# Token rows for the final mixing, x turned first, xT loaded later, and stages of its own for step 0

## The chip, the cores and the metric

The kernel runs on one core of a Trainium2 chip. Its time is the device time of one execution in microseconds (us), and the figure compared is the median over runs. Five engines run their own instruction streams and meet through semaphores: TensorE (PE, with its weight loads as PEld), VectorE (DVE), ScalarE (ACT), GpSimd (POOL) and SyncE (SP), which here only issues DMAs. ACT and POOL issue DMAs as well. The DMA engines, 16 in the profile, carry all transfers.

## The reference

Two branches read the same x (2048 tokens of 1024) and are mixed token by token with a gate `g`. Branch A walks over 64 segments of 32 tokens and carries a memory of 8 rows from segment to segment. Branch B is a GELU-gated feed-forward layer with 3584 hidden columns.

```python
def _A_ref(x, mem0, Wq, Wk, Wv, Wo, seg_len):
    ...
    for s in range(n_seg):
        xs = x[:, s * seg_len:(s + 1) * seg_len, :].copy()
        h = jnp.concatenate([mem, xs], axis=1)
        q = jnp.einsum('btd,dhe->bhte', h, Wq)   # k and v alike; 32 heads of 128
        ...
        scores = jnp.where(mask[None, None], scores, -1000000000.0)
        p = _softmax(scores, axis=-1)
        o = jnp.einsum('bhqk,bhke->bhqe', p, v)
        o = jnp.einsum('bhte,hed->btd', o, Wo)
        mem = o[:, :M, :].copy()
        outs.append(o[:, M:, :])

def _B_ref(x, w_gate, w_up, w_down):
    return _gelu(x @ w_gate) * (x @ w_up) @ w_down
g = _sigmoid((x * gate_w).sum(-1, keepdims=True))
return g * a + (1 - g) * b
```

## The kernel before

The program is a list of operations in one order, written by hand. Each operation goes to one engine; its waits are worked out from the regions that it reads and writes, and each engine runs its own in the order of the list. A DMA has a lane, and a DMA waits for the one before it on its lane. PSUM has 8 banks; two engines that touch the same bank are kept in the order of the list. On-chip memory is laid out by hand in slots of 4 KB a partition, counted by `edge(n)` from 0 to 49, and tiles of different phases share them.

**Head and branch B.** x comes in 16 tiles of 128 tokens (`px`, four buffers). `do_x(T)` turns a tile on TensorE (L550), copies the result to `xT` or `xq` in halves by ACT and DVE (L557, L558), copies the last 8 rows of each segment by DVE (L559), writes both to memory (`xq_scr`, `xr_scr`), and then lets GpSimd multiply the tile with the gate's weights into `gp` (L566) and DVE sum the product (L568). `gate(fb)` makes the gate of four tiles and writes it out, to `g_scr` and, 4 bytes to a row, to `gt_scr` (L636). `load_h` fetches a segment's turned x into `hT`, the input of the recurrence, and a DVE copy puts the memory rows beside it (L663).

The four token blocks `fb` of 512 tokens each have 28 column blocks `j`: 8 matmuls for the gate and 8 for the up projection (L680), then Square and Tanh on ACT (L688, L692) and three operations on DVE (L689, L693, L696). Column block j uses PSUM banks that block j-2 must have left. The gate and up weights come in five chunks `c` of 2, 5, 7, 7 and 7 column blocks (`load_w`). Then comes the down projection, two passes `ps` over seven weight tiles `wd` of 1 MB (L732), 16 matmuls to a tile. The tiles have three buffers: `load_wd` for the tile three ahead is issued when a tile is used up. In the last block all seven tiles, `wdF`, are loaded ahead. `mix` scales the result by 1-g and writes it to `b_scr`. `load_xT(fb+1)` (L594) fetches the next block's 1 MB of turned x. `begin(n)` loads a slot of the recurrence's weights for the first time, and `spread` copies weights within memory.

**The recurrence.** 64 steps, each with the projections k, q, v and the output projection o in two halves of the heads, r = 0 and 1, each in eight pieces n. The walk over (m, r, n) is a list, and `on(m, r, n, f)` hangs work in front of a piece. Weights do not all fit, so `spent` has SP reload the pieces that share a slot. The last 8 rows of each segment and the memory both go through "rest" projections: `fill` (L986) projects the last rows of four segments at a time, `fill_evac` copies the result to a stage by ACT and for v writes it to `v_scr` (L997), and `fill_put` turns it (L814), copies it by DVE (L1009) and writes it to `qk_scr` from GpSimd (L1011, one lane, `fq`). `load_qk` and `load_v` (L581, L585) bring a step's share back, and `put_rest` (L1015) copies it into `kT`. `scores` (L839 to L862) makes the softmax, `attend` (L874) applies it and `rest_o` (L899) collects the rest rows of the output, which go to `o_scr`. A stage is a place under a working tile: stage "k" is kT's, "q" is qT's, "o" is oT's, 0 and 1 lie under hT and oRc. The weights o are `wall`, all others `sl`. After the last output piece `fold` adds the two halves of PSUM: a DVE copy of 64x256 to `part` (L960) and a DVE sum (L961); then TensorE turns the memory rows for the next step (L970). The folded result goes from GpSimd to `a_scr`.

**The mixing.** `oR` holds the rest rows of all steps, four blocks of 1 MB; TensorE multiplies each with Wo (L1157), and DVE adds the gated sum (L1167). For each of 16 token tiles `load_a` fetches branch A's rows from `a_scr` in four DMAs of 96 x 256 (L780) and branch B's from `b_scr` in one (L782); `blend` sums them on DVE (L789) and ACT writes the result (L792). There are six buffers of each (`NA`), and tile T+5 is asked for after tile T's sum.

Of the kernel before, what the change touches and what calls it, by code (L numbers as in the profile page):

```python
# [5 lines left out]
BF16 = mybir.dt.bfloat16  # L6
# [204 lines left out]
def bass_gated_mix__memory_aug_recurrent_mem_tr__geglu_ffn__prompt_kernel(  # L211
# [34 lines left out]
    with ExitStack() as es:  # L246
# [16 lines left out]
        a_scr = nc.dram_tensor("a_scr", [NSEG, 4, SEG, 256], BF16)  # L263
# [254 lines left out]
        assert cur[0] == edge(50) and len(hosts) == 50  # L518
        tp = [al(f"tp{t}", [128, FB], FP32, at=qkr.off + 4 * FB * t) for t in range(2)]
# [21 lines left out]
        def do_x(T):  # L541
# [21 lines left out]
            if T > 0:  # L563
                op("act", lambda e: e.dma_start(xr_scr[T], to.rearrange("p k i c -> p (k i c)")),
                   rd=[to_r], wr=[("D", "xr", T)], lane=f"xv{x2}")
            op("pool", lambda e: e.tensor_tensor(out=gp[:, :], in0=t[:, :], in1=gwb[:, :], op=ALU.mult),  # L566
# [87 lines left out]
        load_w(1)  # L654
        for T in range(TB):
            do_x(T)
            load_x(T + NPX)
        gate(0)
# [3 lines left out]
        load_h(0, "pool")  # L662
        op("dve", lambda e: e.tensor_copy(hT0[:, :, NR:32], memT[:, :].rearrange("p (k c) -> p k c", k=KC)),  # L663
           rd=[memT.r()], wr=[hT0.r()])
# [84 lines left out]
        oR = [al(f"oR{b}", [128, RB, 32], at=slots[home["q", 0, 0]].off + b * SB * 512) for b in range(NBK)]  # L749
# [7 lines left out]
        NA = 6  # L757
# [6 lines left out]
        assert cur[0] <= slots[home["v", 1, 5]].off  # L764
# [12 lines left out]
        def load_a(T):  # L777
            t, w = asb[T % NA], bsb[T % NA]
            for n in range(4):
                op("sp", lambda e, n=n: e.dma_start(t[0:NM, 256 * n:256 * n + 256], a_scr[4 * T:4 * T + 4, n, 0:NR, :]),  # L780
                   rd=[("D", "a", s) for s in range(4 * T, 4 * T + 4)], wr=[t.r(256 * n, 256 * n + 256)], lane=f"al{T % NA}{n}")
# [427 lines left out]
```

## Time and profile before

| | us |
|---|---|
| median of 3 runs | 2300.27 |
| lowest and highest | 2295.94, 2300.56 |
| the profiled execution | 2304.75 |
| its span, first to last instruction | 2302.9 |
| TensorE busy | 2051.2 (89%) |
| DVE, ACT, POOL busy | 1042.1, 539.0, 434.2 |
| mean granted TensorE clock | 0.965 |

The span is read in stretches: head and branch B until about 650 us, the recurrence until about 2180, the mixing until the end. In the profile's rows, a timeline row has start, length, engine, line, operation, what it writes and reads, count, and in brackets how long the engine had been idle and what ended that; a letter q behind an engine's name means its instruction queue, as in SPq for the DMAs that SyncE issues.

### The profile page before, as it was taken

The numbers are of one execution on the slowest core, as the hardware profiler recorded it, in microseconds if no ns is written. First come the engines' busy times: TensorE is split into PE (matmuls) and PEld (weight loads), VectorE is DVE, ScalarE is ACT, GpSimd is POOL, SyncE is SP. The second block draws the span as 40 slices with busy tenths as digits, with TensorE's granted clock in tenths as the row PEclk, the third lists the DMA queues.
The fourth block names the chain that finished last, engine by engine and source line by source line (L and its number), as shares of the span: only waits on it lengthen the run. The fifth ranks groups of instructions, "written<-read, shape, count | busy, mean of one in ns | idle before, by whom it ended". The sixth has DMA issues, their size and how long they took to land.

```text
span 2302.9 us, 69850 instructions
## 1 busy us (share of the span) xinstructions
PE 2051.2 (89%) x31365; PEld 975.8 (42%) x31365; DVE 1042.1 (45%) x2689; ACT 539.0 (23%) x1110; POOL 434.2 (19%) x839
## 2 busy tenths in 40 slices
PE   5999989999968999899999999999999989998880
PEld 2444434444424444444444444444444444444450
DVE  3624606516314445454545454555454544544412
ACT  2312303203112222222222222222222222222100
POOL 3000100000012222222222222222223222221100
PEclk8999999999989999999999999999999999998895
DMA  9255385293577899899999898999999989998932
GB/s 302 107 169 193 107 248 166 59 320 118 188 282 281 329 345 350 330 349 346 346 342 350 330 350 330 358 347 361 351 351 335 349 327 345 342 348 321 345 121 99
DMA packets 187871, 652.74 MB, mean 283 GB/s; under 512 B 22156, under 2 KB 78092, under 8 KB 146740
## 3 DMA queue, kind: packets, MB, share of 16 engines
q1 hardware_dynamic: 161060, 608.10, 72.6%
q0 software_dynamic: 14528, 26.32, 3.5%
q10 hardware_dynamic: 11984, 13.85, 1.7%
q8 instruction: 246, 4.03, 0.7%
q14 instruction: 53, 0.43, 0.1%
HBM read 613.64 MB, written 49.23 MB: 288 GB/s over the span
## 4 chain that ended last, share of the span: by engine, by line
PE 62%; DMA 21%; DVE 6%; SPq 5%; ACT 3%; issue 2%; POOL 1%; ACTq 0%; DVEq 0%; POOLq 0%
PE pb L916 24%; PE pb L680 13%; DMA wall<-o_scr 10%; PE pb L732 7%; PE pb L932 5%; PE pb L814 3%; SPq L780 3%; PE pb L949 3%; DMA o_scr<-oRc 3%; PE pb L986 2%; DMA wd<-in_B_w_down_dram 2%; DMA sl<-v_scr 1%; DVE oT L800 1%; PE pb L874 1%; DMA qk_scr<-1S 1%
## 5 line engine op out<-in xcount | busy, mean ns | idle before, releaser
L916 PE MATMUL pb<-sl,hT 128*32 128x512 bf16 x12288 | 763.9, 384 | 15.1 <-DVE hT L973 8.8
L916 PEld LDWEIGHTS pb<-sl,hT 128*32 128x32 bf16 x12288 | 308.5, 97 | 326.7 <-issue 27.7
L680 PE MATMUL pb<-xT,wg 128*128 128x512 bf16 x896 | 215.2, 384 | 21.8 <-DVE GT L696 15.6
L986 PE MATMUL pb<-sl,hR 128*32 128x512 bf16 x3072 | 212.9, 385 | 3.2 <-DVE osb L621 1.5
L680 PE MATMUL pb<-xT,wu 128*128 128x512 bf16 x896 | 212.3, 380 | 0.0
L949 PE MATMUL pb<-wall,oT 128*32 128x256 bf16 x4056 | 152.8, 280 | 28.0 <-DMA wall<-o_scr 23.7
L899 POOL COPY oRc<-oT 128x128 bf16<-128x128 bf16 x128 | 96.5, 754 | 402.4 <-DVE oT L800 402.4
L960 DVE COPY part<-pb 64x256 f32<-64x256 f32 x128 | 54.0, 422 | 257.4 <-PE pb L949 256.7
L732 PE MATMUL pb<-wd,GT 128*128 128x512 bf16 x672 | 154.1, 393 | 15.4 <-DMA wd<-in_B_w_down_dram 15.4
L932 PE MATMUL pb<-wall,oT 128*32 128x512 bf16 x2048 | 147.2, 386 | 5.8
L688 ACT ACTIVATE s<-pb 128x512 f32<-128x512 f32 x112 | 66.7, 596 | 325.1 <-PE pb L680 291.8
L680 PEld LDWEIGHTS pb<-xT,wg 128*128 128x128 bf16 x896 | 86.9, 99 | 129.0 <-DVE GT L696 21.4
L949 PEld LDWEIGHTS pb<-wall,oT 128*32 128x32 bf16 x4056 | 98.0, 98 | 87.8 <-ACT oT L797 26.7
L689 DVE SCALAR_TENSOR_TENSOR tp<-s,pb 128x512 f32<-128x512 f32 x112 | 76.9, 686 | 128.2 <-ACT s L688 128.2
L680 PEld LDWEIGHTS pb<-xT,wu 128*128 128x128 bf16 x896 | 88.0, 98 | 106.8 <-issue 1.9
L800 DVE COPY kT<-pb 128x512 bf16<-128x512 bf16 x128 | 54.4, 425 | 166.0 <-PE pb L814 165.6
L850 ACT ACTIVATE E<-pb 128x320 bf16<-128x320 f32 x128 | 56.0, 437 | 308.0 <-DVE pb L849 308.0
L797 ACT ACTIVATE oS<-pb 128x512 bf16<-128x512 f32 x65 | 38.8, 597 | 376.4 <-PE pb L916 367.7
L1015 POOL COPY kT<-qkr 128x128 bf16<-128x128 bf16 x128 | 37.3, 291 | 434.6 <-DVE tAB L862 219.3
L862 DVE STREAM_TRANSPOSE tAB<-pAB 128x128 bf16<-128x128 bf16 x512 | 114.1, 280 | 4.4
L693 DVE SCALAR_TENSOR_TENSOR tp<-tp,pb 128x512 f32<-128x512 f32 x112 | 77.0, 687 | 78.1 <-ACT tp L692 77.3
L732 PEld LDWEIGHTS pb<-wd,GT 128*128 128x128 bf16 x672 | 67.1, 101 | 102.0 <-DMA wd<-in_B_w_down_dram 18.6
(106 smaller groups left out, 2201.1 us busy)
## 6 DMA issues: line engine op xcount, KB each, us to landing
sl<-v_scr SPq DMA_DIRECT2D x64, 1536.0 KB, 9.9
wall<-o_scr SPq DMA_DIRECT2D x63, 1536.0 KB, 9.3
wall<-o_scr SPq DMA_DIRECT2D x131, 512.0 KB, 5.1
sl<-k_scr SPq DMA_DIRECT2D x64, 1024.0 KB, 5.5
sl<-q_scr SPq DMA_DIRECT2D x64, 1024.0 KB, 8.2
sl<-v_scr SPq DMA_DIRECT2D x64, 1024.0 KB, 9.4
wd<-in_B_w_down_dram SPq DMA_DIRECT2D x42, 1024.0 KB, 6.3
wdF<-in_B_w_down_dram SPq DMA_DIRECT2D x7, 1024.0 KB, 8.6
```

What stands on the lines that cost most here:

```text
L680: ins = e.matmul(PB[bk][:, 0:FB], lhsT=w[:, kc, cc:cc + 128], rhs=xT[:, :, :, kc, :].rearrange("p t i c -> p (t i) c"), start=(kc == 0), s ...
L689: op("dve", lambda e, hg=hg, t=t: e.scalar_tensor_tensor(out=t[:, :], in0=s1[:, :], scalar=1.0, in1=hg, op0=ALU.add, op1=ALU.mult), rd=[BK ...
L693: op("dve", lambda e, hu=hu, t=t: e.scalar_tensor_tensor(out=t[:, :], in0=t[:, :], scalar=1.0, in1=hu, op0=ALU.add, op1=ALU.mult), rd=[BK( ...
L732: ins = e.matmul(PB[bank[2 * k + hf]][:, :], lhsT=GT[:, j, tb * 128:(tb + 1) * 128], rhs=w[:, x, hf * 512:(hf + 1) * 512], start=(j == 0), ...
L780: op("sp", lambda e, n=n: e.dma_start(t[0:NM, 256 * n:256 * n + 256], a_scr[4 * T:4 * T + 4, n, 0:NR, :]), rd=[("D", "a", s) for s in rang ...
L800: op("dve", lambda e: e.tensor_copy(o, i), rd=rd, wr=wr, after=after)
L862: return [op("dve", lambda e, c=c: e.transpose(tAB[:, c + 32 * k:c + 32 * k + 4 * w].rearrange("p (j x) -> p j x", j=4)[:, :, 0:32], pAB[: ...
L899: op("pool", lambda e: e.tensor_copy(oRc[:, :, 16 * u:16 * u + 16].rearrange("p c x -> p x c"), oT[:, :, :, 32:40].rearrange("p g j c -> p ...
L916: ins = e.matmul(PB[bk][32 * g:32 * g + 32, :], lhsT=h[:, i, :], rhs=w[:, g * 512:(g + 1) * 512], start=(n == 0), stop=(n == 7))
L932: ins = e.matmul(PB[XO][32 * g:32 * g + 32, :], lhsT=oT[:, j, x, 0:32], rhs=wall[:, na:nb + 1:nb - na, c:c + 256], start=(n == 0 and hp == 0),
L949: ins = e.matmul(PB[XO][32 * g:32 * g + 32, 256 * b:256 * b + 256], lhsT=oT[:, j, x, 0:32], rhs=w[:, c:c + 256], start=False, stop=(n % 4 ...
L986: ins = e.matmul(PB[b][32 * g:32 * g + 32, :], lhsT=h[:, k[2], :], rhs=w[:, g * 512:(g + 1) * 512], start=(n == 0), stop=(n == 7))
```

## The change

- `a_scr` is kept in token rows: `[NSEG, SEG, D]` in place of `[NSEG, 4, SEG, 256]`. The store of each step writes four groups of 32 rows by 256 columns to it, and `load_a` fetches a tile in one DMA of 96 x 1024.
- The mixing has 14 buffers in place of 6. `oR` moves to other slots, and its first load stands at (v, 1, 0) of the last step, not at (v, 1, 4).
- `do_x` ends after the turn; the product and the sum are `dot_x`. At the head the four turns come first; the products of tiles 0 to 3, the loads of tiles 4 to 7, the loads of weight chunks 3 and 4 and of the first three `wd` tiles, and the gate follow in the column blocks 0 to 4. `load_w(2)` comes ahead of the turns. `load_h(0)` and its copy go to column block 1 of the last token block. The later turns move from blocks 3, 9, 15, 21 to 6, 11, 16, 21.
- `load_xT` moves from the start of the down projection to its second pass, behind the fourth weight tile's matmuls and in front of that tile's `load_wd`.
- Step 0 has four stages of its own, X0 to X3, in slot 49; its first load of that slot moves into step 0, and the fills, puts, scores and attends of step 0 stand at other places.
- `fold` of the first half copies by ACT, not DVE, in the steps s with s % 4 equal to 0 or 3.

```diff
-        a_scr = nc.dram_tensor("a_scr", [NSEG, 4, SEG, 256], BF16)
+        a_scr = nc.dram_tensor("a_scr", [NSEG, SEG, D], BF16)
...
+        for n in range(4):
+            stage[f"X{n}"] = al(f"X{n}", [128, 512], at=edge(49) + 1024 * n)
...
+        def dot_x(T):
+            t = px[T % NPX]
             op("pool", lambda e: e.tensor_tensor(out=gp[:, :], in0=t[:, :], in1=gwb[:, :], op=ALU.mult),
...
         load_w(1)
+        load_w(2)
         for T in range(TB):
             do_x(T)
-            load_x(T + NPX)
-        gate(0)
         op("pe", tr_mem, rd=[pm.r(), mT.r(), ident.r()], wr=[BK(6)])
...
-        load_h(0, "pool")
-        op("dve", lambda e: e.tensor_copy(hT0[:, :, NR:32], memT[:, :].rearrange("p (k c) -> p k c", k=KC)),
-           rd=[memT.r()], wr=[hT0.r()])
-        load_w(2)
-        load_w(3)
-        load_w(4)
-        for n in range(3):
-            load_wd()
+
+        def begin_h():
+            load_h(0, "pool")
+            op("dve", lambda e: e.tensor_copy(hT0[:, :, NR:32], memT[:, :].rearrange("p (k c) -> p k c", k=KC)),
+               rd=[memT.r()], wr=[hT0.r()])
...
-                T = TB * (fb + 1) + (j - 3) // 6
-                if fb < NFB - 1 and j in (3, 9, 15, 21):
+                if fb == 0 and j < TB:
+                    dot_x(j)
+                    load_x(j + NPX)
+                if fb == 0 and j == TB - 1:
+                    load_w(3)
+                    load_w(4)
+                    for n in range(3):
+                        load_wd()
+                if fb == 0 and j == TB:
+                    gate(0)
+                if fb == NFB - 1 and j == 1:
+                    begin_h()
+                T = TB * (fb + 1) + (j - 6) // 5
+                if fb < NFB - 1 and j in (6, 11, 16, 21):
                     do_x(T)
+                    dot_x(T)
                     load_x(T + NPX)
...
-            if fb + 1 < NFB:
-                load_xT(fb + 1)
-            else:
+            if fb + 1 == NFB:
                 for n in (11, *range(20, 29)):
                     begin(n)
...
                     if not end:
+                        if ps == NPS - 1 and c == 3:
+                            load_xT(fb + 1)
                         load_wd()
                     elif ps == NPS - 1:
                         for n in (29 + 2 * c, 30 + 2 * c, 43 + c):
-                            begin(n)
+                            if n < 49:
+                                begin(n)
...
-        oR = [al(f"oR{b}", [128, RB, 32], at=slots[home["q", 0, 0]].off + b * SB * 512) for b in range(NBK)]
+        oR = [al(f"oR{b}", [128, RB, 32], at=(slots[home["k", 1, 5]].off + b * SB * 512) if b < 3 else slots[home["q", 0, 0]].off) for b in range(NBK)]
...
-        NA = 6
+        NA = 14
...
             t, w = asb[T % NA], bsb[T % NA]
-            for n in range(4):
-                op("sp", lambda e, n=n: e.dma_start(t[0:NM, 256 * n:256 * n + 256], a_scr[4 * T:4 * T + 4, n, 0:NR, :]),
-                   rd=[("D", "a", s) for s in range(4 * T, 4 * T + 4)], wr=[t.r(256 * n, 256 * n + 256)], lane=f"al{T % NA}{n}")
+            op("sp", lambda e: e.dma_start(t[0:NM, :], a_scr[4 * T:4 * T + 4, 0:NR, :]),
+               rd=[("D", "a", s) for s in range(4 * T, 4 * T + 4)], wr=[t.r()], lane=f"al{T % NA}")
...
             pt, cs = part, slice(256 * b, 256 * b + 256)
-            op("dve", lambda e: e.tensor_copy(pt[lo, :], PB[XO][hi, cs]), rd=[BK(XO)], wr=[pt.r()])
+            if b == 0 and s % 4 in (0, 3):
+                act_copy(pt[lo, :], PB[XO][hi, cs], [BK(XO)], [pt.r()])
+            else:
+                dve_copy(pt[lo, :], PB[XO][hi, cs], [BK(XO)], [pt.r()])
...
             fill_evac(m, r, G, b, st)
-            fill_put(m, r, G, st)
...
             if s == 0:
-                on("k", 0, 0, lambda: fill0("k", 0, B0, "k"))
-                if NG > 1:
-                    on("k", 0, 0, lambda: fill0("k", 0, B1, "o", 1, hR1))
-                on("q", 0, 0, lambda: fill0("q", 0, B1, "q"))
-                on("v", 0, 0, lambda: fill0("v", 0, B2, "o"))
+                on("k", 0, 0, lambda: fill0("k", 0, B0, "X0"))
+                on("k", 0, 0, lambda: fill0("k", 0, B1, "X1", 1, hR1))
+                on("k", 0, 0, lambda: fill_put("k", 0, 0, "X0"))
+                on("k", 0, 2, lambda: fill_put("k", 0, 1, "X1", SS))
+                on("q", 0, 0, lambda: fill0("q", 0, B1, "X2"))
+                on("q", 0, 2, lambda: fill_put("q", 0, 0, "X2"))
+                on("v", 0, 0, lambda: fill0("v", 0, B2, "X3"))
...
             if s == 0:
-                on("k", 1, 1, lambda: scores(ua, False))
-                on("k", 1, 1, lambda: attend(ua))
-                on("k", 1, 1, lambda: fill0("k", 1, B0, "k"))
-                on("q", 1, 0, lambda: fill0("q", 1, B1, "q"))
-                on("q", 1, 4, lambda: fill0("v", 1, B2, "k"))
+                on(*('k', 1, 4), lambda: scores(ua, False))
+                on("k", 1, 1, lambda: fill0("k", 1, A1, "X0"))
+                on(*('q', 1, 2), lambda: attend(ua))
+                on("k", 1, 4, lambda: fill_put("k", 1, 0, "X0"))
+                on("q", 1, 0, lambda: fill0("q", 1, B1, "X1"))
+                on("q", 1, 2, lambda: fill_put("q", 1, 0, "X1"))
+                on("q", 1, 4, lambda: fill0("v", 1, B2, "X2"))
+                on("o", 0, 4, lambda: begin(49))
...
-            on(*(("q", 1, 1) if s else ("o", 0, 0)), lambda: evac(bank_of["k", 1], stage[ub if s else "k"], "act"))
+            on("q", 1, 1, lambda: evac(bank_of["k", 1], stage[ub if s else "k"], "act"))
...
-                on("o", 0, 6, lambda: scores(ub, False))
+                on(*('v', 1, 0), lambda: scores(ub, False))
...
-                    on(*((("v", 1, 4), ("o", 1, 0), ("o", 1, 1)) + (("o", 1, 2),) * 3)[n], f)
+                    on(*((("v", 1, 0), ("o", 1, 0), ("o", 1, 1)) + (("o", 1, 2),) * 3)[n], f)
...
-            on("k", 0, 4, lambda: op("pool", lambda e: e.dma_start(a_scr[s].rearrange("g r c -> (g r) c"), a_bf[:, :]), rd=[a_bf.r()],
+            on("k", 0, 4, lambda: op("pool", lambda e: e.dma_start(a_scr[s].rearrange("r (g c) -> g r c", g=4), a_bf[:, :]), rd=[a_bf.r()],
```

More of the change, by code (lines that the diff above doesn't have):

```diff
@@ L747, in bass_gated_mix__memory_aug_recurrent_mem_tr__geglu_ffn__prompt_kernel @@
         assert not copies and not any(done)
-        oR = [al(f"oR{b}", [128, RB, 32], at=slots[home["q", 0, 0]].off + b * SB * 512) for b in range(NBK)]
+        oR = [al(f"oR{b}", [128, RB, 32], at=(slots[home["k", 1, 5]].off + b * SB * 512) if b < 3 else slots[home["q", 0, 0]].off) for b in range(NBK)]
+        assert home["q", 1, 6] == home["k", 1, 5] + 7
         def load_oR(b):
@@ L763, in bass_gated_mix__memory_aug_recurrent_mem_tr__geglu_ffn__prompt_kernel @@
         gR = al("gR", [128, NBK], FP32)
-        assert cur[0] <= slots[home["v", 1, 5]].off
+        assert cur[0] <= edge(19)
         def load_gates():
@@ L1139, in bass_gated_mix__memory_aug_recurrent_mem_tr__geglu_ffn__prompt_kernel @@
         ended = fold(NSEG - 1, 1)
-        op("pool", lambda e: e.dma_start(a_scr[NSEG - 1].rearrange("g r c -> (g r) c"), a_bf[:, :]), rd=[a_bf.r()],
+        op("pool", lambda e: e.dma_start(a_scr[NSEG - 1].rearrange("r (g c) -> g r c", g=4), a_bf[:, :]), rd=[a_bf.r()],
            wr=[("D", "a", NSEG - 1)], lane="st")
```

## The prediction, written before the changed kernel was run

> **What bounds the kernel now.** I read the chain of waits first, then the busy time by stretch, and last the timeline of every place where the tensor engine stops. In the stretches, x counts instructions and the last three columns are the granted clock, the DMA engines' busy share and what they moved.
>
> ```profile
> core 0: us, PE busy (x) PEld busy (x) DVE busy (x) ACT busy (x) POOL busy (x), PEclk, DMA share, GB/s
> 7.00:10.00 3.00, 1.78 (x16) 1.26 (x14) 2.37 (x5) 0.61 (x2) 1.67 (x2) 1.00 1.19 311
> 134.00:142.00 8.00, 8.00 (x38) 3.63 (x37) 1.37 (x2) 0.26 (x1) 0.08 (x1) 1.00 0.42 28
> 145.00:150.00 5.00, 1.54 (x4) 0.59 (x5) 0.00 (x0) 0.00 (x0) 0.00 (x0) 0.67 1.05 391
> 133.80:189.40 55.60, 51.31 (x225) 22.33 (x224) 4.10 (x6) 0.46 (x1) 0.28 (x1) 0.94 0.84 265
> 289.10:347.30 58.20, 51.55 (x225) 22.39 (x224) 4.10 (x6) 0.46 (x1) 0.39 (x1) 0.94 0.82 253
> 448.10:503.50 55.40, 50.92 (x226) 22.46 (x225) 4.10 (x6) 0.44 (x1) 0.00 (x0) 0.94 0.84 271
> 600.20:648.50 48.30, 48.30 (x224) 21.72 (x222) 4.10 (x6) 0.24 (x1) 0.00 (x0) 1.00 0.77 277
> 650.00:711.50 61.50, 40.70 (x671) 17.57 (x674) 13.91 (x39) 10.02 (x20) 14.49 (x26) 0.83 0.59 209
> 750.00:2181.00 1431.00, 1312.46 (x26862) 630.41 (x26854) 706.84 (x2146) 369.85 (x821) 360.59 (x738) 0.99 0.92 343
> 2260.00:2290.00 30.00, 0.00 (x0) 0.00 (x0) 6.45 (x6) 0.00 (x0) 0.00 (x0) 0.50 0.30 102
> ```
>
> The long stretch is the recurrence, 750 to 2181: TensorE is busy 1312.46 of 1431 us with the DMA engines at 0.92, so both are near full, and the change scarcely touches it. It works on what lies outside: the head, three of the four down projections (55.6, 58.2 and 55.4 us where the fourth, whose weights are all there, takes 48.3), step 0 of the recurrence (61.5 us with 40.7 busy), and the mixing at the end, where TensorE has nothing left to do.
>
> **The head.** Now DVE stands still at the copy into hT, and the matmuls behind it:
>
> ```profile
> 15.01 1.22 DVE L568 TENSOR_REDUCE dl<-gp 128x1 f32<-128x1024 f32 x1 [1.70 <-POOL gp L566]
> ...
> 16.62 3.59 PE L680 MATMUL pb<-xT,wg 128*128 128x512 bf16 x8 [5.34 <-DVE xT L558]
> ...
> 21.95 1.89 PE L680 MATMUL pb<-xT,wg 128*128 128x512 bf16 x8
> ...
> 37.25 0.18 DVE L663 COPY hT<-memT 128x64 bf16<-128x64 bf16 x1 [16.89 <-DMA hT<-xq_scr]
> 37.34 0.68 DVE L689 SCALAR_TENSOR_TENSOR tp<-s,pb 128x512 f32<-128x512 f32 x1
> 38.72 0.69 DVE L693 SCALAR_TENSOR_TENSOR tp<-tp,pb 128x512 f32<-128x512 f32 x1 [0.69 <-ACT tp L692]
> ...
> 40.18 3.60 PE L680 MATMUL pb<-xT,wg 128*128 128x512 bf16 x8 [14.61 <-DVE GT L696]
> ```
>
> Two edits act here. The four x turns lose the GpSimd product and its reduction from between them: the first real matmul now waits 5.34 us for the last turn's copy, itself queued behind reductions that wait for GpSimd. It should start near 11.3. And the load of hT with its copy goes to the last block, where GpSimd has nothing ahead of it but DMA issues, so the copy costs its 0.18 us. Column blocks 0 and 1 then take what they take now (16.62 to 21.95 with a cold first group, 5.3 us, then 16 matmuls of 0.216, 3.45: a down projection's 224 take 48.3), so block 2 begins near 20.1 instead of 40.18: 20.1 us, and 1.6 more because block 2 no longer starts cold (3.60 against 1.9). Against it: in blocks 0 to 3 DVE has a reduction more. One block is then three tensor operations of 0.69, 0.69 of wait for the Tanh and 1.22, 4.0 us, on DVE where the matmuls take 3.45; four times 0.55 is 2.2. Gain **19.5**; 14.6 if only the shown wait goes, 22 if DVE catches up. What hides the rest: chunk 2's weights (3.67 MB, 9.4 us at 391 GB/s) are now issued right behind chunk 1's; the 5.8 MB ahead of them end near 21 at 311 to 391 GB/s, so they land near 31 and are used from block 7 at about 39. The gate's small writes come later, at block 4, and hit chunk 3, needed only at about 64.
>
> **xT's load.** At the start of a down projection the queue now holds xT ahead of the next weights:
>
> ```profile
> 129.81 2.12 POOL L636 DMA_DIRECT2D gt_scr<-gal  x4
> ...
> 133.99 0.39 SPq L594 DMA_DIRECT2D xT<-xq_scr  x1
> ...
> 148.46 37.36 PE L732 MATMUL pb<-wd,GT 128*128 128x512 bf16 x160 [4.13 <-DMA wd<-in_B_w_down_dram]
> ```
>
> The excess over 48.3 is 7.3 + 9.9 + 7.1 = 24.3 us: the wait (4.13 in the first) and the half-clock matmuls behind it (0.67 in 145:150). Not all goes. From 134 to 142, behind the gate's writes of 4 bytes a row (L636), the DMA moves 28 GB/s at a busy share of 0.42; after that 391. Those writes stay where they are. The first weight tile, issued 3.45 us into the phase, will sit in that slow stretch in xT's place and land about 12 us in where 10.4 is needed: 1.5 to 2.5 us stay, short enough not to cost the clock, I think. Moved behind the third tile of the second pass, xT is 1 MB (2.7 us at 391) in a stream that has 3.45 us per 1 MB tile, so 0.7 us of stall there, and it lands some 6 us before block 0 of the next phase. Behind it on SP stand the remaining tile loads, which wait for their buffers anyway. Left: about 3.5 + 5.5 + 3.3; gain **12**, bounds 5 and 17.
>
> **Step 0.** The staging tiles of its own remove waits of ScalarE on earlier writes. What stays is the chain on GpSimd:
>
> ```profile
> 666.10 0.75 POOL L1011 DMA_DIRECT2D qk_scr<-qS  x1 [5.55 <-DMA qk_scr<-oS]
> ...
> 673.33 0.56 POOL L581 DMA_DIRECT2D qkr<-qk_scr  x1 [4.29 <-DMA qk_scr<-qS]
> 676.40 0.29 POOL L1015 COPY kT<-qkr 128x128 bf16<-128x128 bf16 x1 [2.51 <-DMA qkr<-qk_scr]
> ...
> 680.98 0.32 PE L874 MATMUL pb<-tAB,vA 32*128 32x40 bf16 x16 [3.69 <-DVE tAB L862]
> ...
> 687.49 0.78 POOL L1011 DMA_DIRECT2D qk_scr<-kS  x1 [4.64 <-DVE kS L1009]
> ...
> 698.92 0.40 PE L814 MATMUL pb<-ident,kS 128*128 128x128 bf16 x4 [4.18 <-ACT kS L797]
> ...
> 711.49 0.82 PE L916 MATMUL pb<-sl,hT 128*32 128x512 bf16 x12
> ```
>
> The three puts to qk_scr share one lane, each waiting for the one before, and the first now comes 1.1 us later, with one more fill ahead of it. So the first scores, which wait for the rest of kT (L1015), come at about 677.8, no sooner than now; TensorE has run on to them and waits some 8 us. But then the fill of k and the first half of k's projection (2.9 us) lie before the scores, and the softmax (3.69 of wait) has the next fill over it: the second put chain starts when DVE is free of the softmax, near 682.5 instead of 687.49. From that put to the next step's matmuls is 24.0 us now; I take off the 4.18 us in which they wait for k's copy (now earlier, and its tile not v's staging) and add 1.5 for half-clock matmuls behind the longer wait. End near 703.8: gain **8**, bounds 3 and 13. The load of slot 49 now waits on SP for the staging tiles' writes (near 693), with the next output weights queued behind it; they are needed near 705, and their 2 MB take 5.4 us at 391, so about 6 us cover it; beyond that each us of delay costs one.
>
> **The mixing.** Three views from 2188 on: the chain of waits by line, the transfers with their sizes and, where it is told, the time to landing, and two of the final sums on DVE, eight tiles apart.
>
> ```profile
> by line: SPq L780 63.3%; SPq L782 16.3%; DMA bsb<-b_scr 7.5%; issue 3.6%; SPq L774 3.1%; DVEq L1174 1.6%; SPq L752 1.0%; DVE bsb L789 0.0%; SPq L143 0.0%
> ```
>
> ```profile
> asb<-a_scr SPq DMA_DIRECT2D x64, 48.0 KB
> bsb<-b_scr SPq DMA_DIRECT2D x16, 192.0 KB
> out_dram<-bsb ACTq DMA_DIRECT2D x16, 192.0 KB
> brb<-b_scr SPq DMA_DIRECT2D x4, 256.0 KB, 7.7
> ```
>
> ```profile
> 2239.55 1.28 DVE L789 SCALAR_TENSOR_TENSOR bsb<-asb,gM,bsb 96x1024 bf16<-96x1024 bf16 x1 [5.70 <-DMA bsb<-b_scr]
> ...
> 2290.71 1.28 DVE L789 SCALAR_TENSOR_TENSOR bsb<-asb,gM,bsb 96x1024 bf16<-96x1024 bf16 x1 [5.70 <-DMA bsb<-b_scr]
> ```
>
> The chain blames SP's issue. I don't believe it. Eight tiles pass in 51.16 us, 6.4 each, and from 2260 to 2290 the DMA engines move 102 GB/s at a share of 0.30, a quarter of the 391 they can. That is what four of sixteen engines give when they are full: SP's issue is slow because the queue ahead is. The three transfers that repeat per tile are the ones for which the view gives no landing, unlike brb's; two of them, b's load and the output, already have rows of 2 KB. [...] The new load of a has the shape of b's load, 4 x 24 rows of 2 KB, so I leave it on a quarter; only its pieces grow from 512 B. The x weights of chunk 0 come in 512 B pieces, 311 GB/s in 7:10 against 391: a tile's 192 KB of a take 2.5 us at a quarter of 311 and 2.0 at a quarter of 391. Sixteen times 0.5 is 8, less a little for what overlaps already: gain **7**, bounds 2 and 11. Fourteen buffers only let SP run further ahead of a full queue.
>
> **Folds, oR, the store.** ScalarE's copy of 256 columns lies between its 160 and 320:
>
> ```profile
> L797 ACT ACTIVATE oT<-pb 128x160 bf16<-128x160 f32 x246 | 61.1, 303 | 31.7 <-PE pb L882 31.7
> ...
> L850 ACT ACTIVATE E<-pb 128x320 bf16<-128x320 f32 x123 | 53.8, 437 | 293.6 <-DVE pb L849 293.6
> L960 DVE COPY part<-pb 64x256 f32<-64x256 f32 x124 | 52.3, 422 | 249.5 <-PE pb L949 248.9
> ```
>
> about 383 ns against 422, and a wait for another engine added: 32 times between -0.15 and +0.1 us, taken as 0. oR's earlier issue stands in the queue behind the last weights: 0. The store of a writes the same 128 pieces of 512 B in other places: 0, bounds below.
>
> **Sum.** 19.5 + 12 + 8 + 7 = 46.5 us off the profiled execution's 2304.75, its span 2302.9: 2258. The median of the three runs, 2300.27, lies 4.5 lower, so I forecast 2254.
>
> **Rivals.** (1) SP's issue is the bound of the mixing after all. Then three quarters of L780's issues go and the mixing ends with TensorE's last group:
>
> ```profile
> 2234.05 4.48 PE L1157 MATMUL pb<-wall,oR 128*128 128x512 bf16 x20
> ```
>
> 2238.5 + 5.5 for the last blend and write = 2244, 59 us sooner: 2202 in all. For it speaks the chain, against it the 0.30. Chance 0.10. (2) The store of a on a quarter of the engines. Its target is now walked 4 x 32, against 128 rows; 64 KB at a quarter of 391 is 0.67 us instead of 0.17, 0.5 us more on four engines in each of 63 steps, while weights stand behind it:
>
> ```profile
> PE pb L949 <- DMA wall<-o_scr: 22.9, 33, 1.7
> ```
>
> In these 33 waits (22.9 us in all) a later landing counts in full, elsewhere it has slack or meets another wait: 17 us at the least, 31 at most; I take 20, 2274. [...] Chance 0.12. (3) Slower: the scattered 512 B pieces stall the DMA as the gate's 4 B pieces do. L636 writes 512 pieces and the DMA is slow for 8 us; 128 pieces, 2 us a step, 63 times: 126 us, 2380. It decides from 46.5 / 63 = 0.74 us a step. Against it: the pieces are 128 times as big. [...] Chance 0.04. (4) Step 0 or the down projections give only their lower bounds, 2266; within my own range.
>
> **Numbers.** The forecast with its bounds has 0.74: gains from 32 to 61 give 2239 to 2268. The range takes in rival 2: 2238 to 2282; it leaves out rivals 1 and 3 and a little more. About 0.2% (4.6 us) is what a measurement can tell from no change. Faster 0.94, same 0.02, slower 0.04.
>
> **What would show it.** Right: block 2 of the first phase near 20, no wait at L663; down projections of 51 to 54 us; step 0 about 53 us; in the mixing DMA shares near 0.3 and some 5.9 us a tile, the end over 45 us behind TensorE's last group. Wrong: a mixing that ends with TensorE (rival 1), steps of the recurrence longer than now's 23.3 us mean with more waits on wall (rival 2), or down projections that still wait 4 us.

## The result, and the profile after

The changed kernel takes **2263.8 us** (median of 4 runs, 2262.5 to 2268.7); the kernel before, run beside it, 2300.4 (2295.9 to 2302.4). The ratio is 0.985, 95% interval 0.983 to 0.987: faster, by 36.6 us. The forecast was 2254 in a range from 2238 to 2282. The profiled execution takes 2268.7 us (span 2266.9) against 2304.75 before, 36.0 us less.

Busy time by stretch of the changed kernel, cut at the same events as before (columns as in the first view of the prediction): the first 8 us of the first down projection, the four down projections, step 0 of the recurrence, the recurrence, and what follows TensorE's last group.

```profile
core 0: us, PE busy (x) PEld busy (x) DVE busy (x) ACT busy (x) POOL busy (x), PEclk, DMA share, GB/s
116.40:124.40 8.00, 8.00 (x38) 3.62 (x38) 1.37 (x2) 0.21 (x1) 0.04 (x1) 1.00 0.30 19
116.37:170.20 53.83, 48.36 (x219) 21.57 (x223) 4.10 (x6) 0.24 (x1) 0.07 (x1) 1.00 0.85 282
271.24:323.69 52.45, 48.44 (x219) 21.56 (x223) 4.10 (x6) 0.23 (x1) 0.07 (x1) 1.00 0.85 283
424.00:476.40 52.40, 48.50 (x220) 21.49 (x223) 4.10 (x6) 0.25 (x1) 0.00 (x0) 1.00 0.86 291
573.30:621.60 48.30, 48.08 (x219) 21.73 (x222) 4.10 (x6) 0.24 (x1) 0.00 (x0) 1.00 0.76 275
623.10:682.40 59.30, 39.24 (x660) 17.40 (x664) 13.22 (x38) 10.50 (x21) 14.51 (x26) 0.86 0.59 217
721.50:2152.50 1431.00, 1309.41 (x26890) 629.01 (x26888) 693.00 (x2116) 381.80 (x852) 371.85 (x739) 0.99 0.93 344
2209.24:2266.92 57.68, 0.00 (x1) 0.00 (x0) 14.84 (x14) 0.00 (x0) 0.00 (x0) 0.54 0.29 105
```

Read the first numbers of the rows against those of before, taken from its trace at the same events (there the first down projection starts at 133.8, the recurrence at 650.0, and step 0 takes 60.9 us until the next step's memory rows are in hT). The first down projection starts at 116.4 instead of 133.8: the head gave 17.4 us. The recurrence starts at 623.1 instead of 650.0, 26.9 sooner: the three phases in between gave 9.5 more. Step 0 (59.3 against 60.9) gave 1.6, the steps behind it 1.8 (mean 23.26 against 23.29), the end of the last step and the border rows' matmuls took 1.0 back (84.7 against 83.7), and the mixing behind TensorE's last group gave 6.7 (57.7 against 64.4). Together 36.0.

The head, TensorE and ScalarE (timeline: start, duration, engine, line, operation, then the idle time before it and what ended it):

```profile
13.54 0.33 ACTq L563 DMA_DIRECT2D xq_scr<-xT  x1
14.40 0.60 ACT L559 ACTIVATE xT<-pb 128x512 bf16<-128x512 bf16 x1 [3.79 <-DMA xq_scr<-xT]
15.51 3.49 PE L680 MATMUL pb<-xT,wg 128*128 128x512 bf16 x8 [4.85 <-DVE xT L560]
24.01 1.89 PE L680 MATMUL pb<-xT,wg 128*128 128x512 bf16 x8
```

Block 2 starts at 24.0 instead of 40.2, and at full clock (1.89 instead of 3.60), as forecast; but block 0 starts only 1.1 us sooner, not 5.3. ScalarE's copy of the fourth tile waits 3.79 us, not for data but behind its own store at 13.54, which waited for an earlier store to land.

Step 0, GpSimd's and TensorE's timelines:

```profile
647.25 0.56 POOL L585 DMA_DIRECT2D qkr<-qk_scr  x1 [3.85 <-DMA qk_scr<-X]
649.75 0.32 PE L854 MATMUL pb<-kT,qT 128*32 128x40 bf16 x16 [7.03 <-POOL kT L1033]
661.71 0.56 POOL L585 DMA_DIRECT2D qkr<-qk_scr  x1
666.64 0.55 POOL L589 DMA_DIRECT2D vB<-v_scr  x1 [4.37 <-DMA v_scr<-X]
667.18 0.56 POOL L580 DMA_DIRECT2D hR<-xr_scr  x1
667.72 0.31 POOL L1033 COPY kT<-qkr 128x128 bf16<-128x128 bf16 x1
668.18 0.32 PE L854 MATMUL pb<-kT,qT 128*32 128x40 bf16 x16 [5.76 <-POOL kT L1033]
673.42 1.47 PE L1004 MATMUL pb<-sl,hR 128*32 128x512 bf16 x12 [4.78 <-DMA hR<-xr_scr]
674.68 3.31 PE L931 MATMUL pb<-sl,hT 128*32 128x512 bf16 x32
```

Three waits of 7.0, 5.8 and 4.8 us are left, and behind them 32 matmuls at half clock (3.31 us at a granted clock of 0.57; the same 32 take 1.90 in the last experiment). The first was forecast; the second and the third are new. In the kernel before, GpSimd issued the same loads in the same order, but SP's loads of output weights came behind them; now they come ahead. The rows of the kernel before, then SP's of the changed one:

```profile
698.53 0.55 POOL L585 DMA_DIRECT2D vB<-v_scr  x1 [0.97 <-DMA v_scr<-kS]
699.07 0.56 POOL L576 DMA_DIRECT2D hR<-xr_scr  x1
699.94 2.77 SPq L430 DMA_DIRECT2D wall<-o_scr  x3
```

```profile
660.38 1.31 SPq L430 DMA_DIRECT2D wall<-o_scr  x2
666.80 0.50 SPq L430 DMA_DIRECT2D wall<-o_scr  x1
```

The load of hR, before and after (the last number is the time from issue to landing, in us):

```profile
hR<-xr_scr POOLq DMA_DIRECT2D x1, 64.0 KB, 2.1
```

```profile
hR<-xr_scr POOLq DMA_DIRECT2D x1, 64.0 KB, 6.2
```

The mixing: two final sums eight tiles apart, and two of SP's issues.

```profile
2206.80 1.28 DVE L804 SCALAR_TENSOR_TENSOR bsb<-asb,gM,bsb 96x1024 bf16<-96x1024 bf16 x1 [5.12 <-DMA bsb<-b_scr]
...
2254.44 1.28 DVE L804 SCALAR_TENSOR_TENSOR bsb<-asb,gM,bsb 96x1024 bf16<-96x1024 bf16 x1 [5.20 <-DMA bsb<-b_scr]
```

```profile
2231.60 2.05 SPq L797 DMA_DIRECT2D bsb<-b_scr  x1
2233.69 3.57 SPq L795 DMA_DIRECT2D asb<-a_scr  x1
```

Eight tiles take 47.64 us, 5.96 each (6.4 before, 5.9 forecast), at a DMA share of 0.29 and 105 GB/s, still a quarter of the 391 GB/s that the prediction read from 145 to 150 us. SP needs 2 to 3.6 us for one issue.

### The profile page after: what moved, and what is told of

It reads as the page before. It is cut to its first block, busy times and chain, and to the rows that moved or that the text cites. A ratio compares the mean times of both kernels' runs of the same rounds, so it can differ in the third digit from the quotient of the medians.

```text
span 2266.9 us, 69748 instructions
## 1 busy us (share of the span) xinstructions
PE 2035.6 (90%) x31339; PEld 971.7 (43%) x31365; DVE 1026.8 (45%) x2657; ACT 551.8 (24%) x1142; POOL 445.1 (20%) x839
## 4 chain that ended last, share of the span: by engine, by line
PE 58%; DMA 26%; DVE 5%; SPq 4%; ACT 3%; issue 2%; POOL 1%; ACTq 0%; DVEq 0%; POOLq 0%
PE pb L931 22%; PE pb L680 14%; DMA wall<-o_scr 13%; PE pb L743 6%; PE pb L947 5%; PE pb L829 3%; DMA o_scr<-oRc 3%; DMA wd<-in_B_w_down_dram 3%; PE pb L964 3%; SPq L795 2%; PE pb L1004 2%; DMA qk_scr<-1S 2%; DMA qk_scr<-0S 1%; DVE oT L815 1%; SPq L797 1%
## 5 line engine op out<-in xcount | busy, mean ns | idle before, releaser
L743 PE MATMUL pb<-wd,GT 128*128 128x512 bf16 x657 | 145.8, 379 | 13.5 <-DMA wd<-in_B_w_down_dram 12.7
L815 DVE COPY part<-pb 64x256 f32<-64x256 f32 x96 | 40.4, 421 | 249.9 <-PE pb L964 249.9
L815 DVE CAST oT<-pb 128x160 bf16<-128x160 f32 x256 | 76.3, 319 | 71.2 <-PE pb L897 71.2
```

Of the source, the lines that this page charges most:

```text
L743: ins = e.matmul(PB[bank[2 * k + hf]][:, :], lhsT=GT[:, j, tb * 128:(tb + 1) * 128], rhs=w[:, x, hf * 512:(hf + 1) * 512], start=(j == 0), ...
L815: op("dve", lambda e: e.tensor_copy(o, i), rd=rd, wr=wr, after=after)
```

## The experiments

Each kernel was timed beside the kernel before on the same chip, where that took 2290 to 2299 us. In their profiles the steps behind step 0 took between 1430 and 1450 us in all, although few of the edits touch anything there. Total times therefore don't tell edits of a few us apart. The stages can, but each kernel has one profile, so a stage too is good to a few us only.

**The mixing: buffers, layout, order of rows.** Three kernels. `u_na6` is the changed kernel with `NA = 6`; `u_mix` has that and the old groups of a; `e_rows` is the changed kernel with another order of rows:

```
- a_scr[4 * T:4 * T + 4, 0:NR, :]
+ a_scr[4 * T:4 * T + 4, 0:NR, :].rearrange("s r d -> r s d")
  (the same for b's load, the output and gM's load)
```

> The changed kernel with the mixing alone put back: rows of a in four groups of 256 columns, four loads of 512 B pieces per tile, six buffers, and the old store of a. Theory (a quarter of the DMA engines bounds the mixing, and larger pieces shorten it): a tile takes 6.4 us again instead of 5.9, the end lies about 64 us behind TensorE's last group instead of 57.7, and the median is 2264 + 7 = 2271. Rival (the new store of a costs time in every step): the steps get shorter with the old store, 63 times about 0.3 us, so the mean step falls from 23.26 to about 22.9 us and the time to about 2250.

> The changed kernel with six instead of fourteen buffers for the mixing, the row layout kept. Theory (the queue of four engines is full either way): nothing changes, 5.9 us a tile, the end 57 to 58 us behind TensorE's last group, median 2264. Rival (the fourteen buffers brought the mixing's gain): the end moves back to about 64 us behind TensorE, median 2271.

> The changed kernel with the rows of a mixing tile ordered row first, segment second (24 x 4 instead of 4 x 24), in both loads, the output and the gate's column; the same bytes and as many instructions. [...] Rival (SP's issue, some 6 us a tile, is the bound): no change, 2264.

Measured: u_mix 2270.4 (ratio 0.991, 0.988 to 0.994), 63.3 us behind TensorE's last group; u_na6 2260.9 (0.988, 0.985 to 0.991), 55.6 us behind; e_rows 2206.9 (**0.964**, 0.960 to 0.969), 3.9 us behind. The stretches behind TensorE's last group in that order, and for e_rows also one beside it:

```profile
2213.99:2277.29 63.31, 0.00 (x0) 0.00 (x0) 16.73 (x16) 0.00 (x0) 0.00 (x0) 0.52 0.30 100
```

```profile
2203.18:2258.80 55.62, 0.00 (x0) 0.00 (x0) 14.84 (x14) 0.00 (x0) 0.00 (x0) 0.55 0.29 105
```

```profile
2195.17:2199.10 3.93, 0.00 (x1) 0.00 (x0) 0.75 (x1) 0.00 (x0) 0.00 (x0) 0.77 0.13 33
2165.00:2195.00 30.00, 30.00 (x140) 19.87 (x138) 17.06 (x16) 0.00 (x0) 0.00 (x0) 1.00 0.65 231
```

So the 6.7 us came from the new layout of a (pieces of 2 KB instead of 512 B, and one load to a tile instead of four; these runs don't separate the two), and the eight more buffers bring nothing. What bounds the mixing is the shape of its transfers: with 24 x 4 rows in place of 4 x 24 the same bytes, in as many instructions, move at 231 GB/s beside TensorE and the tail is gone. No view tells the DMA engines apart: that it is their number was an estimate from the rates, 102 and 105 of 391 GB/s, and is not shown. In e_rows SP's long issues are gone too, so they had come from the full queue:

```profile
2158.29 0.76 SPq L795 DMA_DIRECT2D asb<-a_scr  x1
2159.09 0.76 SPq L797 DMA_DIRECT2D bsb<-b_scr  x1
```

u_mix also has the old store of a. Its steps are not shorter: mean 23.39 us. The three kernels with the old store (before, b_gt, u_mix) have 23.25 to 23.39 us a step, mean 23.31, the eleven with the new one 23.07 to 23.37, mean 23.25. TensorE's waits for output weights (us in all, times, longest), of the changed kernel and of u_mix:

```profile
PE pb L964 <- DMA wall<-o_scr: 27.3, 39, 2.1
```

```profile
PE pb L965 <- DMA wall<-o_scr: 30.8, 39, 2.3
```

**xT's load.** `u_xt` puts the one call of `load_xT` back to the start of the down projection.

> The changed kernel with xT's load alone put back to the start of each down projection. Theory (xT stood in the slow stretch ahead of the first new weight tile): the three down projections take about 56 us instead of 52.9 on average, 10 us more in all, median 2274. Rival (the stretch behind the gate's writes costs the same whatever stands first in the queue): the down projections stay at 52 to 54 us, median 2264.

Measured: 2263.2 (0.988, 0.984 to 0.991); the three down projections 53.3, 55.1 and 52.5 us, 160.9 together. Nine kernels that have xT late and the gate's stores lie between 152.7 and 158.7, mean 155.7: xT's place is worth about 5 us, half of what the theory wanted. The kernel before took 169.1, so some 8 us of it hang on something else. The first tile's wait in the three phases of u_xt was 3.18, 3.21 and 3.07 us; the four us behind each (the third number from the end is the granted clock):

```profile
130.00:134.00 4.00, 3.93 (x11) 1.46 (x12) 0.00 (x0) 0.00 (x0) 0.00 (x0) 0.59 1.04 385
283.00:287.00 4.00, 3.54 (x9) 1.29 (x10) 0.00 (x0) 0.00 (x0) 0.00 (x0) 0.57 1.04 384
438.00:442.00 4.00, 3.18 (x15) 1.49 (x16) 0.00 (x0) 0.00 (x0) 0.00 (x0) 1.00 1.05 388
```

Two of three waits of nearly the same length cost the clock: 0.59 over four us is some 3.3 us at half clock, which costs some 1.6 us beside the wait itself.

**The gate's stores.** `e_gt` takes the sixteen stores of 4 B a row (L640) out of the changed kernel, `b_gt` out of the kernel before; in both, sixteen small loads at the end read the border rows' gate from g_scr:

```
- for T in range(TB * fb, TB * fb + TB):
-     op("pool", ... e.dma_start(gt_scr[4 * T:4 * T + 4, :, :]..., gal[:, T:T + 1]) ...)
...
- e.dma_start(gR[0:RB, b:b + 1], gt_scr[SB * b:SB * b + SB, NR:SEG, :])
+ for t in range(TB):
+     e.dma_start(gR[32 * t:32 * t + 32, b:b + 1], g_scr[:, TB * b + t:TB * b + t + 1].rearrange("(n r) o -> n r o", n=4)[:, NR:SEG, :])
```

> The changed kernel without the gate's sixteen transposed stores of 4 B a row (L640); the border rows' gate is read at the end from g_scr, in sixteen loads of 32 values. What is left of the gate is one store of 16 B a row per phase. Theory (those 4 B writes hold the whole DMA up for some 8 us ahead of each down projection): between the gate and 8 us into a down projection the DMA moves over 200 GB/s instead of 19, the first waits of the three down projections (2.3, 1.7, 1.8 us) vanish, the three take 50 to 51 us each instead of 52.9, some 7 us less in all. Rival (any small store does it, the 16 B one too): waits and 52.9 us stay.

> The kernel before (none of the change) without the gate's sixteen stores of 4 B a row; the border rows' gate is read at the end from g_scr, in sixteen small loads. Theory (these stores are what the head and the down projections of the kernel before wait for, and the change gains there by not standing right behind them): hT's load, issued at some 21 to 24 us, lands within 6 us instead of 14, block 2 starts at 27 to 30 us instead of 40.2; the three down projections take 51 to 53 us instead of 55.6, 58.2 and 55.2; the mixing loses some 6 us by the small loads; in all 10 to 20 us less than before, ratio 0.991 to 0.995. Rival (the weights queued ahead of hT's load make it late, and xT's load makes the down projections late): block 2 stays near 40, the down projections at 55 or more, the time is 5 us longer by the small loads.

Measured: e_gt 2271.9 (0.992, 0.988 to 0.995); the first waits of the three down projections are gone, though the one store of 16 B a row is still there, so the rival is refuted. The three take 50.1, 49.4 and 50.2 us, 9 us less than in the changed kernel's profile. The DMA moves 133 GB/s in the first 8 us, not over 200, as SP issues the first weight tile only 3.4 us into them. The mixing takes 64.2 us instead of 57.7; the sixteen loads stand ahead of the first tiles on SP:

```profile
2151.04 10.79 SPq L783 DMA_DIRECT2D gR<-g_scr  x16
```

By these two stages that is a gain of some 2 us; the times show none, the ratio is even above the changed kernel's 0.985, and why is open. b_gt: 2276.5, **0.991** (0.988 to 0.994) of before. Its DVE copy into hT, its down projections, and the first 8 us of the first:

```profile
26.28 0.18 DVE L659 COPY hT<-memT 128x64 bf16<-128x64 bf16 x1 [5.91 <-DMA hT<-xq_scr]
```

```profile
123.73:172.08 48.35, 48.35 (x226) 21.91 (x225) 4.10 (x6) 0.46 (x1) 0.00 (x0) 1.00 0.86 305
271.71:321.76 50.05, 48.52 (x226) 21.83 (x225) 4.10 (x6) 0.46 (x1) 0.00 (x0) 1.00 0.84 294
421.54:469.92 48.38, 48.38 (x226) 21.82 (x225) 4.10 (x6) 0.46 (x1) 0.00 (x0) 1.00 0.88 311
124.00:132.00 8.00, 8.00 (x39) 3.64 (x38) 1.38 (x2) 0.19 (x1) 0.00 (x0) 1.00 0.71 265
```

hT's load, issued at 21.2 with the weights queued ahead of it as ever, lands in 5 us instead of 14, and block 2 starts at 29.2 instead of 40.2. The three down projections take 146.8 us instead of 169.1, with xT's load still at their start: it lands in 5.6 to 5.9 us instead of 11.7 to 12.7. That is less than e_gt's 149.7 with xT moved: without these stores the new place of xT seems no better than the old one, by one profile each.

How much of the time do the sixteen stores, 2 KB a phase, account for? By the two profiles the recurrence starts 33 us sooner (616.6 instead of 650.0), but the profiles come from two chips. Beside each other on one chip the kernels differ by 18.6 us, to which the 6.4 us that the mixing lost are to be added (70.8 us against 64.4): some 25 us, 20 to 34 by the interval. The whole change got 26.9 there.

**hT's load.** `u_h` puts `begin_h()` back ahead of block 0 and leaves the gate behind block 4.

> The changed kernel with the load of hT and DVE's copy into it put back ahead of column block 0; the gate of phase 0 stays behind block 4. Theory (the load takes its 14 us from issue to landing because the weights are in the queue ahead of it): it is issued at about 14 us, when the first store of x has landed, DVE stands still behind it until 25 us or later, and column block 2 starts at 30 us or later instead of 24.0: 6 us or more of the 16 lost again. Rival (in the kernel before it landed late because the gate's 4 B writes stood ahead of it on GpSimd and held up the DMA): it lands within some 6 us, by 20, and block 2 starts within 3 us of 24.0.

Measured: 2267.1 (0.985, 0.982 to 0.988).

```profile
18.11 0.18 DVE L667 COPY hT<-memT 128x64 bf16<-128x64 bf16 x1 [3.30 <-DMA hT<-xq_scr]
```

Block 2 starts at 24.3 against 24.0. The rival holds: the load lands in 5.3 us, and moving it to the last block gave nothing once the gate's stores came behind it. The b_gt run, where the weights are queued as before, adds that the weights were not what held it up.

**The head's stores.** `e_lanes` gives each of the first four tiles lanes of its own: `lane=f"xw{T if T < TB else x2}"`, and so for xv.

> The changed kernel with a lane of its own for each of the first four tiles' stores of x (four lanes for xq_scr, four for xr_scr, instead of two each). Theory (ScalarE, which issues these stores in order, waits at tile 2's store until tile 0's has landed, and so brings its copy of the fourth tile late): the first matmul of column block 0 starts near 11.5 us instead of 15.5, block 2 near 21.5 (its up weights land then) instead of 24.0, and the first down projection 2.5 to 4 us sooner than at 116.4. Rival (DVE, which has a reduction more in each of the first blocks, sets the pace whatever the start): block 0 earlier, but the down projection within 1 us of 116.4.

Measured: 2254.8 (0.984, 0.980 to 0.987).

```profile
13.17 3.59 PE L680 MATMUL pb<-xT,wg 128*128 128x512 bf16 x8 [2.41 <-DVE xT L560]
```

Block 0 starts 2.3 us sooner, block 2 at 22.8 (1.2 sooner), the down projection at 114.6 instead of 116.4. Half of what was expected: the lane was one of two limits. The copies then follow one another at 2 us a tile, ScalarE's waiting for DVE's of the tile before.

**Step 0.** `e_fq` gives each put of step 0 a lane of its own; `e_ord` issues the load of the border columns (L585) and of hR (L580) ahead of v's four stores:

```
- wr=[("D", "qk", G, m, u)], lane="fq")
+ wr=[("D", "qk", G, m, u)], lane=f"fq{m}{u}" if G < 1 else "fq1" if G < 2 and (m, u) == ("k", 0) else "fq")
```
```
- on("q", 1, 4, lambda: fill0("v", 1, B2, "X2"))
- on("q", 1, 4, lambda: (load_qk(0, 1), load_v(0, slice(1, 2)), load_r(1) if NG > 1 else None))
+ on("q", 1, 4, lambda: fill0("v", 1, B2, "X2", first=(lambda: load_qk(0, 1), lambda: load_r(1))))   # between the fill and its stores
+ on("q", 1, 4, lambda: load_v(0, slice(1, 2)))
```

> The changed kernel with a lane of its own for each of step 0's five puts to qk_scr (one lane for all before). Theory (the first scores wait for the third put, which waits for the landing of the second, and that for the first, 6 us each): the third put is issued about 5 us after the phase's first put instead of 12.7, TensorE's wait of 7.0 us at the first scores shrinks to 1 us or less, and step 0 takes 53 us instead of 59.3. Rival (the puts land slowly because their 256 B pieces are slow, and overlapping them only makes each land later): the wait stays over 4 us, step 0 57 us or more.

> The changed kernel with another order on GpSimd in step 0: the load of the border columns for the second half (L585) and the load of hR (L580) are issued ahead of the four stores of v and the load of v, not behind them. Theory (in the second half both the second scores, 5.8 us, and the fill behind them, 4.8 us plus half-clock matmuls, wait for loads that stand behind v's store and 2.5 MB of output weights): the second scores come 3 to 4 us sooner, no wait for hR over 1 us is left, step 0 takes 50 to 53 us instead of 59.3. Rival (the DMA queue is shared, so the loads land no sooner whatever their place on GpSimd): step 0 58 to 60 us.

Measured: e_fq 2260.2 (0.987, 0.984 to 0.990), step 0 54.4 us; e_ord 2260.3 (0.987, 0.983 to 0.990), step 0 54.5. Nine kernels with an untouched step 0 lie between 58.0 and 60.9. In e_fq the wait at the first scores is 3.25 us instead of 7.03: the puts overlap, but the load behind them now takes some 6 us to land, so theory and rival each have a half. In e_ord the wait for hR is gone, but the second scores still wait 6.9 us and come no sooner in the step (45.2 us into it, 45.1 in the changed kernel): I had left the load of v, which waits for v's stores to land, ahead of the copy into kT on GpSimd.

**The folds.** `u_fold` puts the fold copies back to DVE.

> The changed kernel with the fold copies of steps 0 and 3 of each four put back from ScalarE to DVE. Theory (the copy lies beside other work either way): the mean step stays within 0.1 us of 23.26, the median within 5 us of the changed kernel's, neither told from noise. Rival (the fold copy is on the path): the steps behind s % 4 = 0 and 3 take 0.1 us or more longer than the changed kernel's 23.46 and 22.98, the others as before.

Measured: 2267.9 (0.987, 0.985 to 0.989); mean step 23.31, by s % 4 23.41, 23.89, 23.10 and 22.78 where the changed kernel has 23.46, 23.67, 22.89 and 22.98. The steps that the edit doesn't touch (the second and third number) move more than the others: nothing to be told.

**All together.** `best` joins e_rows, e_lanes, e_fq, e_gt and e_ord with v's load behind the copy into kT.

> [...] Theory (the parts lie in different stages and add): head 2 us less, down projections 9, step 0 some 12 (both waits for kT and the one for hR shrink, 47 to 49 us in all), the mixing 50 (its sixteen small gate loads now stand beside a queue that is not full): 2255 - 73 = about 2182, 0.953 of before. Rival (step 0's two edits share one cause and don't add, and the small gate loads delay the first tiles of the mixing): 2195 or more.

Measured: **2198.6** (2192.8 to 2200.5), 0.956 of before (0.954 to 0.959), against e_rows' 0.964. Step 0 and what follows TensorE's last group:

```profile
615.84:664.04 48.20, 37.10 (x660) 16.91 (x664) 13.35 (x38) 10.49 (x21) 14.35 (x26) 0.96 0.73 263
2184.41:2190.96 6.55, 0.00 (x0) 0.00 (x0) 2.75 (x4) 0.00 (x0) 0.00 (x0) 0.83 0.45 138
```

Step 0 is down from 59.3 to 48.2 us: 11.1, where e_fq and e_ord brought 4.9 and 4.8 singly, so the edits add, with v's load moved as well. In its second half the wait for hR is 1.69 us and the matmuls behind it run at full clock:

```profile
654.56 0.83 PE L1003 MATMUL pb<-sl,hR 128*32 128x512 bf16 x12 [1.69 <-DMA hR<-xr_scr]
655.22 1.90 PE L930 MATMUL pb<-sl,hT 128*32 128x512 bf16 x32
```

The first down projection starts at 114.5, as in e_lanes; the three take 51.1, 50.7 and 51.2 us, a us more each than in e_gt; what follows TensorE takes 6.6 us behind the sixteen small loads instead of e_rows' 3.9. The time is above the 2195 from which the rival was to hold, but that number was reckoned for another chip. The changed kernel's ratio of 0.985 would be 2264 on this chip, so the edits bring 65 us, between the theory's 73 and the rival's 60; e_rows alone would bring 47 of them. In each of the three down projections a wait of 1.7 us at a weight tile behind xT is left.

## Why the prediction was right or wrong

**Head, 19.5 forecast, 17.4 measured.** The size came out near, in part by luck, and the reason was half wrong. I read the wait of 16.89 us at L663 as a matter of where hT's load is issued. u_h refutes that; b_gt shows that the gate's stores ahead of the load made it late, and without them, everything else as before, the first down projection starts 10 us sooner (123.7). The prediction named these stores as slow in the next part and did not apply them here. Two sizes were off and partly cancel. Block 2 starts at 24.0, not near 20.1: of the 5.34 us of wait ahead of block 0 only 0.5 went, because ScalarE, freed of the wait for GpSimd, met the landing of its own stores, and the prediction had not looked at ScalarE's queue. And DVE's reductions, put at 2.2 us, hardly show: the stretch from block 2 to the down projection takes 92.4 us against 93.6 before, where the warm start alone was to save 1.6.

**Down projections, 12 forecast, 10.4 measured** (169.1 to 158.7; in the other kernels 155.7 on average). The forecast excess over 48.3 of 3.5 + 5.5 + 3.3 came out as 5.5 + 4.2 + 4.1. The mechanism held in half: the first wait is 2.27, 1.67 and 1.78 us (1.5 to 2.5 forecast) and costs no clock in this profile (granted 1.00 behind each; in u_fold the 16 matmuls behind a wait of 2.53 us take 5.21 us, at full clock 3.63), but u_xt shows that xT's place is worth only some 5 us. With xT back at the start the waits are 3.1 to 3.2 us, where the kernel before has 4.1 to 5.1, and why is open. That the sum came near is luck to that extent. xT (it stands behind the fourth tile; the prediction says third) costs a wait of 2.99, 0.58 and 1.70 us at a tile behind it instead of 0.7. The other phases' column blocks took 1.0 us longer. The cause of most of the excess, the gate's stores, was seen and left where it was: b_gt takes 22 of the 24.3 us away.

**Step 0, 8 forecast, 1.6 measured: the term that failed.** In the nine kernels with this step 0 it takes 59.6 us on average, against 60.9 and 61.9 in the two without it (before, b_gt). The first half went as told (first scores 26.7 us into the step, 27.8 forecast), and the second chain began 6 us sooner, 5 forecast. From its first put to the next step I had 21.3 us; it took 27.8. I took off the 4.18 us in which TensorE had waited for k's copy, and let the rest of that stretch move along as before. But that wait had held back the output projection, and with it SP's load of the next output weights, until the small loads of GpSimd were out. Now weights are issued from 660.38 on, and the small transfers run beside them. The first of v's four stores, issued at 659.53, still lands in 1.8 us; the other three take 4.2 to 5.2, where all four took 1.8 before. The border columns take 5.2 instead of 2.2, and hR, whose load stands behind that of v and so behind v's stores, is issued at 667.18, right behind more weights, and takes 6.2 instead of 2.1. So the second scores wait 5.76 us, the fill waits 4.78 more for hR, and what follows runs at half clock (0.57). That the weights slow the small transfers is read from the two traces; no run moves the weights alone. e_ord, which issues the two loads ahead, takes the wait for hR away; best, with the load of v behind the copy as well and e_fq's lanes, has step 0 at 48.2. The chain of puts on one lane, seen and accepted as it was, costs 5 (e_fq).

**Mixing, 7 forecast, 6.7 measured.** Right in size, and in cause as far as the runs go: u_na6 and u_mix separate the layout of a from the buffers, though not the size of the pieces from the number of loads, and e_rows has the same bytes in another shape at 231 GB/s. The quarter of the engines is an estimate from 102 of 391 GB/s, and no run shows how many engines a transfer gets. Rival 1 is refuted: SP's issue falls to 0.76 us as soon as the queue isn't full.

**Folds and the store of a, 0 forecast.** u_fold and u_mix show nothing to the contrary; 17 us (rival 2) would be 0.27 us a step, and the mean step is 23.25 us over the kernels with the new store against 23.31 with the old one, while the quarter of the engines that this rival reckoned with is shown by no run; rival 3's 2 us a step is nowhere.

The sum, 46.5, was 10.5 over the measured 36.0: 6.4 of it from step 0, 2.1 from the head, 2.5 from the three phases, 0.3 from the mixing, less the 0.8 that the other steps and the end brought unforeseen.

## What to carry to other kernels

A stall that ends with a transfer can belong to whatever stands in the DMA's way, not to the load that is waited for (hT's took 13.9 us to land behind the gate's 4 B stores, some 5 without them): look for small stores in the us before, and take them out once, before you move the waiting loads. When issues grow long at a low DMA share, try the same bytes in another order of rows (here 24 x 4 in place of 4 x 24: an issue of SP took 0.76 us instead of 2 to 3.6, the stretch behind TensorE 3.9 us instead of 57.7). When a wait is taken away, list what the freed engine will trigger sooner (here a load of weights) and which small transfers that will meet (here hR's load, 6.2 us to landing instead of 2.1), since the next wait will name those.

## What the runs showed of the hardware

Four GpSimd stores of 512 B each, in pieces of 4 B, hold up the core's other transfers: behind them the 1 MB of xT takes 11.7 to 12.7 us to land in the kernel before, without them 5.6 to 5.9 (b_gt). All sixteen in the changed kernel:

```profile
L640 POOL DMA_DIRECT2D gt_scr<-gal x16: 537/537/572, 39.5 to 421.4; - x16
...
DMA to landing us min/median/max: 8.5/10.6/13.4
```

In the first 8 us of its first down projection the DMA moved 19 GB/s; without these stores 133 (e_gt) and 265 (b_gt, where SP has xT to load from the start).

A wait of 2.5 to 3 us sometimes halves TensorE's clock and sometimes doesn't, and the length alone does not decide. The same weight tile's 16 matmuls, late in the first down projection, in u_fold and in the changed kernel:

```profile
165.33 5.21 PE L743 MATMUL pb<-wd,GT 128*128 128x512 bf16 x16 [2.53 <-DMA wd<-in_B_w_down_dram]
```

```profile
166.74 3.63 PE L743 MATMUL pb<-wd,GT 128*128 128x512 bf16 x16 [2.99 <-DMA wd<-in_B_w_down_dram]
```

Behind the shorter wait they take 1.58 us more, some 3.2 us at half clock; behind the longer one the granted clock is 1.00. In the kernel before, the 8 matmuls behind a wait of 2.46 us (L1157, at 2181.72) take 3.27 us at a granted clock of 0.58. What decides between the two is not shown.
